# Additions moved from VectorE to GpSimd in a convolution and MLP kernel whose matmuls use seven products

## The chip, the cores and the metric

The kernel runs on one core of a Trainium2 chip. The metric is the device time of one execution in microseconds (us). The time before is the median of three runs. The five engines of the core each run their own stream of instructions in order and wait for each other by semaphores: TensorE (PE in the profile, its weight loads PEld), VectorE (DVE), ScalarE (ACT), GpSimd (POOL) and SyncE (SP), which only issues transfers here. GpSimd issues transfers too.

## The reference

The input x has the shape (8, 4224, 192) in float32. First comes a causal convolution over the sequence: the 192 channels form 8 heads of 24, each head has 7 taps, and the taps of a head go through a softmax.

```python
w = exp(weight - max); w = w / (sum(w) + 1e-9)            # (8 heads, 7 taps)
out[b, s, h, g] = sum_k w[h, k] * x_pad[b, s + k, h, g]    # 6 zeros stand ahead of x
```

Then an MLP with a layer norm ahead of it works on each row y of 192 numbers (w_ch1 is 192 x 768, w_ch2 is 768 x 192):

```python
xn = (y - mean(y)) / sqrt(var(y) + 1e-6) * g_ln
result = y + maximum(xn @ w_ch1, 0) @ w_ch2
```

## The kernel before

**Groups.** The rows are cut into 18 groups of up to 2048 rows, 16 rows (J) on each of the 128 partitions. Groups 0 and 1 run plainly. For group 2 only the second matmul, and for groups 3 to 17 (MIXED) both matmuls, are computed by seven products of quarters instead of eight, with sums and differences of quarters ahead of and behind the products. The division by the standard deviation is put off: the first weights are centred, and `rstd` multiplies the result of the second matmul.

**Convolution.** The taps of a group are added on VectorE two groups ahead of its matmuls or one: `first_tap` and `second_tap` run on ScalarE (line 380, 398), the second tap's addition is a transfer from tb to y that adds as it lands (line 409, issued by GpSimd), and `conv` (line 417) adds the taps from 2 to 6, head by head, one instruction of 128x384 for each tap and head. `transpose` (line 428) then brings y into yt for TensorE, and `moments` (line 448) takes the statistics.

**First matmul, `up_mixed(g)`.** It runs the seven products twice: a small pass (`one`, a third of the features: index PAIR) and a large pass (`two`, the other two thirds). X and Y are the two halves of the PSUM banks, used in turn: a product into X can begin only when ScalarE has copied X's last result out (`evict`, line 651). A quarter that is the sum of two results is closed by `close`: either VectorE adds PSUM to it (line 657), or ScalarE copies the second result to a free place and a transfer issued by GpSimd adds it (line 609). The free place for the small pass's c21 is `two.c22[:, 0:1]`, which the large pass later writes with its own c22; so that eviction waits until the transfer has landed. The large pass uses parts_cs and parts_tb as free places.

**Second matmul, `down_fast(g)`.** Its seven products (line 850) are called P0 to P6 here. P0 to P3 read the quarters as they are, after `lower_sum` (line 826: a10 = max(a10, 0) - a00, one VectorE instruction for each of three feature indices). P4, P5 and P6 read what three times three half sums (line 817) make of them: P4 reads the first three, and of those the one with index PAIR first, which is made last. ScalarE copies the products into cs and parts (line 856); the parts lie where a10 was. After P6 the next group begins at once.

**Behind the products.** The results of group g-1 are completed in `finish_fast` (line 908), which the generator `ahead` calls in the middle of `up_mixed(g)`: VectorE adds parts to cs (line 912) and transposes six blocks of cs into ot (line 914); ScalarE multiplies by rstd (line 929), and GpSimd issues the transfers that add ot to the output (line 940).

**Order.** The order is written out by hand; nothing reorders it. Each engine keeps the order in which the program names its instructions. What matters of it here:

- VectorE, in a group: taps of the next group, `lower_sum` of index PAIR, three more taps, the closing addition of line 657, the other two `lower_sum`, nine taps, the transpose to yt, nine half sums, three additions from PSUM (line 890), the sums of y s1 and s2 (lines 600 and 601), 16 statistics, then the two additions and six transposes of `finish_fast`.
- GpSimd: the four issues of line 409, the sums of y s3 and s4 (lines 605 and 606), in every second group a memset (line 164), then the transfers that close c11, c22 and c21 of the small pass and those of the large pass. In groups 4, 6, ... 16 (and in 17) `root` (lines 460 to 483) computes rstd for two groups: nine operations on 128x32 elements between the closings of c11 and c22, and ten between those of c22 and c21.

In `up_mixed` this is the piece around the last products:

```python
        p.product(Y, s1, p.b12, False, False)
        taps_of_next(2, 5)
        taps_of_next(5, 6, heads=(0, H // 2))
        p.close(p.c22, Y, None if last else rooms[1][:, 0:PAIR])
        p.product(X, a22, p.t[2], False)
```

Of the kernel before, what the change touches and what calls it, by code (L numbers as in the profile page):

```python
# [11 lines left out]
ALU = mybir.AluOpType  # L12
# [4 lines left out]
def kernel(  # L17
# [29 lines left out]
    nc = tc.nc  # L47
    PSUM = bass.MemoryType.PSUM
    B, S, D = x.shape
    H, K = weight.shape  # L50
# [35 lines left out]
    CH = NC // 2  # L86
# [38 lines left out]
    def take_set():  # L125
        i = (turn[0] + 3) // 4 * 4 % 8
        turn[0] = i + 4
        return all_banks[:, i : i + 4]
# [482 lines left out]
    def up_mixed(g, ahead, pending):  # L611
# [65 lines left out]
                conv(g + 1, *args, **kw)  # L677


        X, Y = take_set(), take_set()  # L680
        one, two = Pass(PAIR, FC, X, Y), Pass(0, PAIR, Y, X)
        p = one
        p.product(X, a11, p.b11, True, False)
        p.evict(X, p.c11)
        p.product(Y, a12, p.b21)
        p.close(p.c11, Y, two.c12[:, 0:1])
        next(pending, None)
        p.product(X, s2, p.t[0], False, False)
        p.evict(X, p.c21)
        p.product(Y, s3, p.t[1], True, False)  # L690
        p.evict(Y, p.c22)
        p.product(X, s1, p.b12, False, False)
        p.close(p.c22, X, two.c12[:, 1:2])
        next(pending, None)
        p.product(Y, a22, p.t[2], False)
        p.close(p.c21, Y, two.c22[:, 0:1])
        p.product(X, s4, p.b22, False)
        p.evict(X, p.c12, True)

        next(ahead)  # L700
        p = two
        rooms = parts(cpool, "cs"), parts(bpool, "tb")
        p.product(Y, a11, p.b11, True, False)
# [37 lines left out]
        if last:  # L741
            one.relu(one.c22)
        else:
            lower_sum(g, (PAIR,))
            taps_of_next(5, 6, heads=(H // 2, H - 1))
        p.close(p.c21, X)
        if last:
            lower_sum(g, (PAIR,))
# [5 lines left out]
        if last:  # L754
# [9 lines left out]
                nc.scalar.activation(kept[:, f, :, :, h], src, AF.Relu)  # L764

            keeping = [lambda f=f, h=h: keep(f, h) for f in range(NF) for h in range(2)]
        taps_of_next(5, 6, heads=(H - 1, H))
        taps_of_next(6, K)

        def scale_one(j):  # L770
# [47 lines left out]
                a[:, *dst, f], a[:, *left, f], a[:, *right, f], op=op  # L818
            )

    def lower_sum(g, fs=range(FC)):

        a = of_products(g)
        if g in MIXED:
            for f in fs:
                nc.vector.scalar_tensor_tensor(
                    out=a[:, 1, 0, f], in0=a[:, 1, 0, f], scalar=0.0, in1=a[:, 0, 0, f],
                    op0=ALU.max, op1=ALU.subtract,
                )
        else:  # L830
            half_sum(g, (1, 0), (1, 0), (0, 0), ALU.subtract, fs)

    def down_fast(g, work):
        n = fast[g]
        t = width(g)
        w = n * T
        a = of_products(g)
        flat = cpool.tile([P, NC, NFAST * C], F32, tag="cs", name=f"cs{g}")[:, :, 0 : n * C]
        order = "p c (h j t) -> p c h j t" if t == C else "p c (j h t) -> p c h j t"
        cs = flat.rearrange(order, h=2, t=t)  # L840
        free = a[:, 1, 0].rearrange("p f q j t -> p (f q) j t")
        parts = [free[:, 0:CH], free[:, CH : 2 * CH]]
        banks = [take_bank() for c in range(CH) for i in range(2)]

        def product(bank, left, right, to, first, behind=0):
            for c in range(CH):
                dst = banks[2 * c + bank]
                for f in (PAIR, *range(PAIR)):
                    for q in range(NQ):
                        nc.tensor.matmul(  # L850
                            dst[C * q : C * q + C, 0:w], right[:, f, C * c : C * c + C],
                            left[:, f, q], start=(first and f == PAIR), stop=(f == PAIR - 1),
                            skip_group_check=True,
                        )
                if to is not None:
                    nc.scalar.copy(  # L856
                        to[:, c], dst[:, 0:w].rearrange("p (j t) -> p j t", t=t)
                    )
                for one in work[:behind]:
                    one()  # L860
                del work[:behind]

        b = quarters_of_w2()
        c11, c21 = cs[:, 0:CH, 0], cs[:, 0:CH, 1]
        c12, c22 = cs[:, CH:NC, 0], cs[:, CH:NC, 1]
        if g == 2:
            work += [lambda h=h: first_tap(4, heads=(h, h + 1)) for h in range(7, H)]
            work += [lambda h=h: second_tap(4, heads=(h, h + 1)) for h in range(H)]
        elif g + 2 < NG:
            work += [  # L870
                lambda tap=tap, h=h: tap(g + 2, heads=(h, h + 1))
                for tap in (first_tap, second_tap) for h in range(H)
            ]
        behind = (1, 1, 1, 1) if g == 2 else (3, 2, 2, 3)
        if g + 1 == NG:
            behind = (0, 0, 1, 2)
        product(0, a[:, 0, 0], b[0], c11, True, behind[0])
        product(1, a[:, 1, 0], w2sums[:, 2], c22, True, behind[1])
        product(1, a[:, 1, 1], w2sums[:, 3], c21, False, behind[2])
        product(1, a[:, 0, 1], b[2], None, True, behind[3])  # L880
        if g + 1 < NG:
            transpose(g + 1)
            if g == 2:
                b11, b12 = quarters_of_w1()[0:2]
                nc.vector.tensor_tensor(b12, b12, b11, op=ALU.subtract)
        half_sum(g, (1, 1), (1, 1), (1, 0), ALU.add)
        half_sum(g, (0, 0), (1, 1), (0, 0), ALU.add)
        half_sum(g, (0, 1), (0, 1), (1, 1), ALU.subtract)
        for c in range(CH):
            nc.vector.tensor_tensor(  # L890
                c11[:, c], c11[:, c], banks[2 * c + 1][:, 0:w].rearrange("p (j t) -> p j t", t=t),
                op=ALU.add,
            )
        product(0, a[:, 1, 1], w2sums[:, 1], parts[0], False, 2)
        product(0, a[:, 0, 0], w2sums[:, 0], parts[1], False, 2)
        for one in work:
            one()
        product(0, a[:, 0, 1], b[3], c12, False)
        if g + 1 < NG:
            sums_of_y(g + 1, nc.gpsimd)  # L900
            if g == 2:
                load_x(5, gate=True)
            moments(g + 1)
        else:
            finish_fast(g, 0, flat, cs, parts)
        return flat, cs, parts

    def finish_fast(g, half, flat, cs, parts):
        n = fast[g]
        ot = ots[g] if half else out_tile(g)  # L910
        fresh = cs[:, CH * half : CH * half + CH, 1]
        nc.vector.tensor_tensor(fresh, fresh, parts[half], op=ALU.add)
        for c in range(CH * half, CH * half + CH):
            nc.vector.transpose(
                ot[:, 0:n, C * c : C * c + C], flat[:, c].rearrange("p (j t) -> p j t", t=C)
            )

    ots = {}

# [76 lines left out]
    def ahead(g):  # L996


        if results is not None:
            for half in range(2):  # L1000
                finish_fast(g - 1, half, *results)
        yield

    w11, w12, w21, w22 = quarters_of_w1()
    b11, b12, b21, b22 = quarters_of_w2()
# [100 lines left out]
```

## Time and profile before

| what | before |
|---|---|
| time, median of 3 runs (lowest to highest) | 955.75 us (955.62 to 957.78) |
| the profiled execution's own time | 956.96 us |
| its span | 954.6 us |
| TensorE busy | 946.8 us, 99% |
| VectorE busy | 894.2 us, 94% |
| ScalarE busy | 694.8 us, 73% |
| GpSimd busy | 341.8 us, 36% |
| one steady group: first matmul, second matmul | 27.96 us, 27.44 us |
| one tap on VectorE, 128x384 | 615 ns, next one 0.53 us later |
| VectorE, two inputs of 128x768, in place (L912) | 929 ns |
| GpSimd, two inputs of 128x768 (L605) | 1831 ns |

The span runs from the first to the last instruction of the profiled execution. L609 means line 609 of the kernel before. In the timeline, a line gives the start, the time that a run of like instructions took (both in us), the engine, the line, what is written and read, shapes and count; in brackets stands how long the engine was idle before, and who ended that wait.

### The profile page before, as it was taken

The page shows a single profiled execution, that of the slowest core. Times are in us where ns is not written, and L with a number is a line of the kernel's source. Part 1 is how long each engine was busy: PE and PEld are TensorE (multiplying, and loading weights), DVE is VectorE, ACT ScalarE, POOL GpSimd, SP SyncE. Part 2 cuts the span into 40 slices and gives each one's busy share as a digit, 9 for nine tenths or more (in the row PEclk, how much of TensorE's full clock was granted, in tenths as well). Part 3 has the DMA queues.
Part 4 walks back from the last instruction along what each step waited for, and adds up shares of the span by engine and source line. Part 5 has one row for each costly group of instructions (what it writes and reads, how often), then busy time and mean ns, then how long its engine had stood idle before and what let it go on. Part 6 is the DMA issues. An engine that isn't in the chain of part 4 may idle for free.

```text
span 954.6 us, 37896 instructions
## 1 busy us (share of the span) xinstructions
PE 946.8 (99%) x16858; PEld 734.5 (77%) x16858; DVE 894.2 (94%) x1496; ACT 694.8 (73%) x1166; POOL 341.8 (36%) x474
## 2 busy tenths in 40 slices
PE   8999999999999999999999999999999999999998
PEld 7998896877869687786958778695867769586787
DVE  8999999999999999999999999999999999999867
ACT  7764678596877959687796968779695877967362
POOL 1158422613145141533227141452316232261330
PEclk9999999999999999999999999999999999999999
DMA  8359589689696988979697897969889697778261
GB/s 206 111 151 218 110 233 269 122 188 226 130 273 131 251 158 185 221 130 278 126 252 152 199 215 128 277 133 249 158 198 206 124 275 134 174 135 141 40 122 68
DMA packets 39832, 169.34 MB, mean 177 GB/s; under 512 B 4469, under 2 KB 8182, under 8 KB 33655
## 3 DMA queue, kind: packets, MB, share of 16 engines
q0 software_dynamic: 32864, 106.77, 60.2%
q1 hardware_dynamic: 6800, 60.16, 17.4%
q8 instruction: 132, 2.16, 0.9%
q14 instruction: 30, 0.25, 0.1%
q10 hardware_dynamic: 6, 0.00, 0.0%
HBM read 38.93 MB, written 50.33 MB: 94 GB/s over the span
## 4 chain that ended last, share of the span: by engine, by line
PE 96%; DMA 1%; POOL 1%; ACT 1%; issue 0%; DVE 0%; ACTq 0%; POOLq 0%
PE ps L533 46%; PE ps L850 44%; PE ps L787 4%; PE ps L367 1%; DMA room<-room 1%; DMA out_dram<-y 1%; PE ps L326 1%; ACT room L651 0%; POOL room L609 0%; POOL d L460 0%; ACT y L380 0%; POOL r L483 0%; POOL d L478 0%; POOL d L479 0%; PE ps L335 0%
## 5 line engine op out<-in xcount | busy, mean ns | idle before, releaser
L417 DVE SCALAR_TENSOR_TENSOR y<-xg,taps,y 128x384 f32<-128x384 f32 (+3 forms) x720 | 364.8, 583 | 2.6 <-DMA y<-room 1.4
L850 PE MATMUL ps<-room,w2sums 128*32 128x256 f32 (+2 forms) x4608 | 246.6, 371 | 0.0
L533 PE MATMUL ps<-yt,w 32*128 32x256 f32 (+2 forms) x4104 | 234.7, 378 | 1.0 <-ACT room L523 0.5
L533 PEld LDWEIGHTS ps<-yt,w 32*128 32x128 f32 x4104 | 204.2, 185 | 26.3 <-issue 8.7
L651 ACT COPY room<-ps 128x1024 f32<-128x1024 f32 (+1 forms) x129 | 169.0, 1310 | 74.5 <-PE ps L533 73.5
L850 PEld LDWEIGHTS ps<-room,w2sums 128*32 128x32 f32 x4608 | 149.3, 110 | 91.5 <-ACT room L664 5.3
L850 PE MATMUL ps<-room,w 128*32 128x256 f32 (+2 forms) x3456 | 188.9, 371 | 0.0
L817 DVE TENSOR_TENSOR room<-room 128x1024 f32<-128x1024 f32 (+2 forms) x147 | 161.2, 1170 | 22.6 <-PE ps L850 16.0
L850 PEld LDWEIGHTS ps<-room,w 128*32 128x32 f32 x3456 | 110.7, 110 | 70.3 <-DVE room L657 5.0
L533 PE MATMUL ps<-ysums,w1sums 32*128 32x256 f32 x2160 | 124.9, 379 | 0.2 <-issue 0.2
L533 PEld LDWEIGHTS ps<-ysums,w1sums 32*128 32x128 f32 x2160 | 109.5, 185 | 10.5 <-ACT room L651 3.3
L940 POOL DMA_DIRECT2D out_dram<-ot x69 | 59.0, 942 | 155.6 <-ACT ot L929 102.5
L409 POOL DMA_DIRECT2D y<-tb x59 | 52.5, 1386 | 153.5 <-ACT room L856 110.1
L856 ACT COPY cs<-ps 128x256 f32<-128x256 f32 (+2 forms) x192 | 70.1, 367 | 45.2 <-PE ps L850 45.2
L664 ACT ACTIVATE room<-room 128x1024 f32<-128x1024 f32 (+1 forms) x89 | 92.5, 1072 | 1.7 <-DMA room<-parts_cs 0.9
L929 ACT ACTIVATE ot<-ot,r 128x192 f32<-128x192 f32 x224 | 90.9, 464 | 0.0
L380 ACT ACTIVATE y<-xg,taps 128x384 f32<-128x384 f32 (+3 forms) x141 | 73.0, 607 | 1.0 <-DMA out_dram<-y 0.7
L448 DVE BATCH_NORM_STATS2 st<-y 128x6 f32<-128x192 f32 x264 | 70.1, 344 | 0.0
L856 ACT COPY room<-ps 128x256 f32<-128x256 f32 (+2 forms) x96 | 35.5, 370 | 45.8 <-PE ps L850 43.8
L398 ACT ACTIVATE tb<-xg,taps 128x384 f32<-128x384 f32 (+1 forms) x120 | 66.1, 628 | 0.0
L533 PE MATMUL ps<-yt,w1sums 32*128 32x256 f32 x1080 | 65.2, 380 | 0.6 <-ACT room L651 0.6
L533 PE MATMUL ps<-ysums,w 32*128 32x256 f32 x1080 | 64.5, 376 | 0.0
(119 smaller groups left out, 924.8 us busy)
## 6 DMA issues: line engine op xcount, KB each, us to landing
xg<-in_x_dram SPq DMA_DIRECT2D x14, 2112.0 KB, 16.4
room<-room POOLq DMA_DIRECT2D x45, 512.0 KB, 5.1
out_dram<-ot POOLq DMA_DIRECT2D x59, 384.0 KB, 9.6
y<-tb POOLq DMA_DIRECT2D x58, 384.0 KB, 8.4
out_dram<-y SPq DMA_DIRECT2D x13, 1536.0 KB, 8.8
room<-parts_cs POOLq DMA_DIRECT2D x28, 512.0 KB, 6.7
room<-parts_tb POOLq DMA_DIRECT2D x14, 1024.0 KB, 7.6
xg<-in_x_dram POOLq DMA_DIRECT2D x1, 2112.0 KB, 13.8
```

What stands on the lines that cost most here:

```text
L380: nc.scalar.mul(y[g][:, 0:n, cs], xg[g][:, 0:n, cs], taps[:, h, 0:1])
L398: nc.scalar.mul(tb[g][:, 0:n, cs], xg[g][:, 1 : 1 + n, cs], taps[:, h, 1:2])
L417: nc.vector.scalar_tensor_tensor(out=y[g][:, 0:n, cs], in0=t[:, k : k + n, cs], scalar=taps[:, h, k : k + 1], in1=y[g][:, 0:n, cs], op0=AL ...
L448: nc.vector.bn_stats(out=sums[g][:, j, :], in_=y[g][:, j, :])
L533: nc.tensor.matmul(banks[:, q, i * w : i * w + w], right[rows, c, P * i : P * i + P], left[rows, :, c, :], start=(first and c == 0 and i = ...
L651: nc.scalar.activation(dst, src, AF.Relu) if relu else nc.scalar.copy(dst, src)
L664: nc.scalar.activation(c, c, AF.Relu)
L817: nc.vector.tensor_tensor(a[:, *dst, f], a[:, *left, f], a[:, *right, f], op=op)
L850: nc.tensor.matmul(dst[C * q : C * q + C, 0:w], right[:, f, C * c : C * c + C], left[:, f, q], start=(first and f == PAIR), stop=(f == PAI ...
L856: nc.scalar.copy(to[:, c], dst[:, 0:w].rearrange("p (j t) -> p j t", t=t))
L929: nc.scalar.mul(ots[g][:, j, :], ots[g][:, j, :], rstd[g][:, j : j + 1])
L940: nc.gpsimd.dma_start(out=rows[:, d0:d1], in_=src[:, d0:d1], accum_op=ALU.add)
```

## The change

1. `add_parts` takes the two additions of parts to cs out of `finish_fast`; in all groups but the last they run on GpSimd at the end of `down_fast`, one ahead of and one behind the sums s3 and s4.
2. The six transposes become a generator that is advanced one step after each eviction of the small pass, and drained after it. In the last group it is only drained.
3. `lower_sum` of index PAIR runs on GpSimd, as a clamp at zero and a subtraction, in all groups of seven-product first matmuls but the last.
4. The three taps that stood between that `lower_sum` and the closing addition (line 657) now stand behind that addition.

```diff
+        def some_of_last():
+            if not last:
+                next(ahead, None)
+
         X, Y = take_set(), take_set()
         one, two = Pass(PAIR, FC, X, Y), Pass(0, PAIR, Y, X)
         p = one
         p.product(X, a11, p.b11, True, False)
         p.evict(X, p.c11)
+        some_of_last()
         p.product(Y, a12, p.b21)
         p.close(p.c11, Y, two.c12[:, 0:1])
+        some_of_last()
         next(pending, None)
...
         p.product(Y, a22, p.t[2], False)
         p.close(p.c21, Y, two.c22[:, 0:1])
+        some_of_last()
         p.product(X, s4, p.b22, False)
         p.evict(X, p.c12, True)
 
-        next(ahead)
+        for _ in ahead:
+            pass
         p = two
...
         if last:
             one.relu(one.c22)
         else:
-            lower_sum(g, (PAIR,))
-            taps_of_next(5, 6, heads=(H // 2, H - 1))
+            lower_sum(g, (PAIR,), nc.gpsimd)
         p.close(p.c21, X)
...
-        taps_of_next(5, 6, heads=(H - 1, H))
+        taps_of_next(5, 6, heads=(H // 2, H))
         taps_of_next(6, K)
...
-    def lower_sum(g, fs=range(FC)):
+    def lower_sum(g, fs=range(FC), engine=nc.vector):
 
         a = of_products(g)
         if g in MIXED:
             for f in fs:
+                if engine is nc.gpsimd:
+                    low = a[:, 1, 0, f]
+                    engine.tensor_scalar(
+                        out=low, in0=low, scalar1=0.0, scalar2=0.0, op0=ALU.max, op1=ALU.add
+                    )
+                    engine.tensor_tensor(low, low, a[:, 0, 0, f], op=ALU.subtract)
+                    continue
                 nc.vector.scalar_tensor_tensor(
...
         product(0, a[:, 0, 1], b[3], c12, False)
         if g + 1 < NG:
+            add_parts(0, cs, parts, nc.gpsimd)
             sums_of_y(g + 1, nc.gpsimd)
+            add_parts(1, cs, parts, nc.gpsimd)
             if g == 2:
                 load_x(5, gate=True)
             moments(g + 1)
...
-    def finish_fast(g, half, flat, cs, parts):
+    def add_parts(half, cs, parts, engine):
+        fresh = cs[:, CH * half : CH * half + CH, 1]
+        engine.tensor_tensor(fresh, fresh, parts[half], op=ALU.add)
+
+    def transposes_of_last(g, half, flat, cs, parts):
         n = fast[g]
         ot = ots[g] if half else out_tile(g)
-        fresh = cs[:, CH * half : CH * half + CH, 1]
-        nc.vector.tensor_tensor(fresh, fresh, parts[half], op=ALU.add)
         for c in range(CH * half, CH * half + CH):
             nc.vector.transpose(
                 ot[:, 0:n, C * c : C * c + C], flat[:, c].rearrange("p (j t) -> p j t", t=C)
             )
+            yield
+
+    def finish_fast(g, half, flat, cs, parts):
+        add_parts(half, cs, parts, nc.vector)
+        for _ in transposes_of_last(g, half, flat, cs, parts):
+            pass
...
         if results is not None:
             for half in range(2):
-                finish_fast(g - 1, half, *results)
-        yield
+                yield from transposes_of_last(g - 1, half, *results)
```

More of the change, by code (lines that the diff above doesn't have):

```diff
@@ L689, in up_mixed @@
         p.evict(X, p.c21)
+        some_of_last()
         p.product(Y, s3, p.t[1], True, False)
         p.evict(Y, p.c22)
+        some_of_last()
         p.product(X, s1, p.b12, False, False)
         p.close(p.c22, X, two.c12[:, 1:2])
+        some_of_last()
         next(pending, None)
@@ L696, in up_mixed @@
         p.close(p.c21, Y, two.c22[:, 0:1])
+        some_of_last()
         p.product(X, s4, p.b22, False)
         p.evict(X, p.c12, True)
-        next(ahead)
+        for _ in ahead:
+            pass
         p = two
```

## The prediction

> **What bounds it.** I read the page first: busy times, then the chain that ended last.
>
> ```profile
> PE 946.8 (99%) x16858; PEld 734.5 (77%) x16858; DVE 894.2 (94%) x1496; ACT 694.8 (73%) x1166; POOL 341.8 (36%) x474
> ...
> PE 96%; DMA 1%; POOL 1%; ACT 1%; issue 0%; DVE 0%; ACTq 0%; POOLq 0%
> ```
>
> TensorE is without work for 7.8 us of 954.6; by the table by stretches 3.1 of them fall in the first 30 us, 0.8 between 117.2 and 894.3 (groups 3 to 16), the rest at the very end. VectorE's 94% is nobody's bound. So taking work off VectorE can return almost nothing; the question is which result for TensorE comes later. The chain in order of time shows groups of exactly 27.96 + 27.44 = 55.40 us and one disturbance:
>
> ```profile
> 671.86 27.96 PE ps L533 x504
> 699.82 27.44 PE ps L850 x504
> ...
> 741.88 6.76 DMA room<-room
> ...
> 748.74 1.88 ACT room L651
> 750.61 0.04 issue
> 750.66 5.46 PE ps L533 x96
> ```
>
> In group 14 the transfer closing the small pass's c21 (L609), issued last behind `root`'s operations on GpSimd, landed 6.76 us later and held ScalarE's eviction, which held TensorE: the stage took 28.86 by the table by stretches, 0.90 more. A weak spot to remember. The timeline of the end of group 11's first matmul and of its second one:
>
> ```profile
> 586.07 0.86 POOL L609 DMA_DIRECT2D room<-parts_tb  x1 [6.85 <-ACT parts_tb L651]
> 586.56 2.29 DVE L657 TENSOR_TENSOR room<-room,ps 128x2048 f32<-128x2048 f32 x1 [0.85 <-PE ps L533]
> 588.95 2.36 DVE L826 SCALAR_TENSOR_TENSOR room<-room 128x1024 f32<-128x1024 f32 x2
> 591.23 4.85 DVE L417 SCALAR_TENSOR_TENSOR y<-xg,taps,y 128x384 f32<-128x384 f32 x9
> 596.21 3.38 DVE L428 STREAM_TRANSPOSE yt<-y 128x3072 f32<-128x3072 f32 x1
> 600.61 10.31 DVE L817 TENSOR_TENSOR room<-room 128x1024 f32<-128x1024 f32 x9 [1.03 <-PE ps L850]
> 604.62 7.95 PE L850 MATMUL ps<-room,w2sums 128*32 128x256 f32 x144
> ```
>
> VectorE waits twice: 0.85 for TensorE before the closing addition (L657), 1.03 before the half sums (L817). P4, the matmul at 604.62, reads the third half sum first; that ends at 600.61 + 3 x 1.146 + 0.06 = 604.1 (10.31/9 = 1.146), and VectorE to TensorE takes 0.1 (588.85 to 588.95). So 0.42 is spare.
>
> [...]
>
> ```profile
> 72.21 9.02 DVE L417 SCALAR_TENSOR_TENSOR y<-xg,taps,y 128x384 f32<-128x384 f32 x12
> 71.27 3.16 POOL L582 TENSOR_TENSOR w2sums<-w 128x288 f32<-128x288 f32 x2
> 74.51 2.07 POOL L582 TENSOR_TENSOR w2sums<-w,w2sums 128x288 f32<-128x288 f32 x2
> ```
>
> Twelve taps cost 12 x 0.53 = 6.4 elsewhere (28 in 14.87); beside four GpSimd additions of 288 elements, 9.02: 0.65 lost for each. [...] Trace: 768 elements take 1.83 (L605) against 0.95 (L600) for two inputs; of one input only 32-element operations are there (0.21).
>
> **Part 1: lower sum to GpSimd, three taps behind the closing.** Leaves VectorE: one L826, 1.2 us, before L657; worth nothing, VectorE waited 0.85 there and will now wait about 3. The three taps (1.6) that also stood before L657 now stand behind it, where the spare is 1.03: 0.57 late at the half sums, so 0.57 - 0.42 = 0.15 of TensorE.
>
> On GpSimd: a clamp and a subtraction of 1024 elements, behind the parts_tb issue, which ends at 586.93. Subtraction: from 0.25 at 32 elements to 1.83 at 768, 2.15 ns each, so 2.4. Clamp, one input: estimate 1.1[...]; bounds 1.1 and 2.4. It runs 586.95 to 588.05 beside L657, which has one SBUF input, the other in PSUM. The subtraction starts at 588.05, [...]and VectorE's first L826, due at 588.95, waits 1.4. P1 wants the result at 592.85 (588.95 + 3.90): in time. Behind it on GpSimd stand only the stores of the rows of ot, first issued at 593.16: not delayed. The half sums are then 1.4 + 1.6 - 1.03 = 1.97 late, P4 1.97 - 0.42 = **1.5 us** in each odd group 3 to 15.
>
> **Part 2: the two additions to GpSimd.** VectorE loses 2 x 0.93 (L912) per group, again before a wait. GpSimd gains 2 x 1.83, the same shape as L605. They enter here (group 14; its start S is 727.19):
>
> ```profile
> 724.77 1.83 POOL L605 TENSOR_TENSOR ysums<-yt 128x768 f32<-128x768 f32 x1 [0.46 <-PE ps L850]
> 726.68 1.82 POOL L606 TENSOR_TENSOR yt<-yt,ysums 128x768 f32<-128x768 f32 x1
> 728.44 1.05 POOL L164 MEMSET xg<- 1x1152 f32 x1
> 731.44 0.90 POOL L609 DMA_DIRECT2D room<-room  x1 [1.95 <-ACT room L651]
> ```
>
> Both wait for ScalarE's copies of the parts, the last of which ends at S-3.4 (L856, 612.64 + 0.37 in group 11, whose successor starts at 616.39): no wait. The first comes after the y<-tb issues (to S-2.9) and meets VectorE's sums of y (L600, L601, two SBUF inputs): one of them waits, so L605 starts at about S-0.3 instead of S-2.4. L605 and L606 end at S+3.4, wanted by TensorE at about S+4.1 and S+8.3 (s3 by 1.9, s4 by L606): hidden. The second addition ends at S+5.2. Before even groups the memset follows: S+6.3. Behind it queue the c11 closing (before S+4.25), nine `root` operations, the c22 closing (S+8.4), ten more, the c21 closing (S+14.69). In odd groups there is no `root`: c11 closes 1 us late, c21 at S+9.9 as before; free.
>
> In even groups the queue is full. Nine operations took 3.5 (732.05 to 735.53) because seven ran beside one-input transposes; beside taps their pitch is 0.55 (735.57 to 741.88 for ten and an issue, 6.3). VectorE's transposes wait for the second addition, so its taps start at S+7.3 to 7.7 (before S+7.1), and about seven operations run slowly: S+6.3, issue 0.6, 4.4 to 5, then 6.3: c21 is issued at S+17.7 (3 later). Landing took 4.65 in a quiet case (187.7, group 4), 6.76 in group 14; with the parts_cs transfers now right behind it I take 5.3: S+23.0. The eviction that waits for it normally starts at S+20.45, so 2.6 late, and group 14 shows 1.09 late cost 0.90: **2.5 us** per even group 4 to 16. Bounds: 1.4 (issue at S+17.3, landing in 4.65) and 4.2. There parts_tb is issued some 0.95 ahead of L657 instead of 0.5, which shortens part 1 to **1.0**.
>
> **Part 3: order of the transposes.** Their order in VectorE's stream does not change (nothing else of VectorE's stands in the small pass, except in the last group, where the generator is drained at the old place): 0, bounded by the 1.9 that half of them take, covered by VectorE's wait of 3 us at L657.
>
> **Sum.** 7 x 1.5 + 7 x (1.0 + 2.5) - 0.9 already paid = 34. The last group keeps its sum on VectorE: 0. Profiled span 954.6 becomes 989; that execution took 956.96, 1.2 above the median, so I add 34 to the median 955.75: **990**.
>
> **Rivals.** (a) One of the two stalls alone, 22%: c21 lands in time (+21, 977), or part 1 is only 0.15 and part 2 whole (+19, 975). For: each hangs on slacks of 0.4 to 1.2. Against: the queue's extra work is certain. (b) The clamp is as slow as the subtraction, or L657 counts as a contender: two holds instead of one, 3.1 in odd and 2.6 in even groups: 7 x 3.1 + 7 x 5.1 - 0.9 = 56, 1012; 17%. No large one-input operation is in the trace to exclude it. (c) Not slower, 6%: GpSimd's long operations don't hold VectorE at L826 and L600. Then part 1 is 0.15 x 14 = 2.1, s3 starts at S-2, c21 is issued at S+15.9 and lands at S+20.5, no later than needed: about 957. It decides if the hold at L826 is below 0.42 - 0.15 = 0.27 us; the 0.65 per 288 elements speaks against it. (d) Faster, 2%: the 0.8 us between 117.2 and 894.3 is all that these edits could return.
>
> **How the numbers follow.** The rest, 53%, is the forecast, its own range 980 to 1000. 968 leaves (c), (d) and a corner of (a) below; 1014 leaves the half of (b) where both holds are long above. A measurement here tells changes over 0.3% (2.9 us) from none: faster 0.02, within 0.06, slower 0.92.
>
> **What would show it.** L843's first instruction starts after GpSimd's subtraction ends, not 2.39 after L657's start; L827 no longer waits for TensorE; P4 (L867) waits for VectorE. In even groups L651 waits for room<-room by some 2.5 us, and the third L609 is issued near S+17.7. VectorE waits about 3 us before L657. Wrong if P4 starts 15.67 after P0 as now, or if the c21 closing stays near S+15.

## The result, and the profile after

| what | before | after |
|---|---|---|
| time, median of 4 runs (lowest to highest), same chip | 956.22 us (955.62 to 957.78) | 1015.0 us (1012.72 to 1019.61) |
| ratio, 95% interval | | 1.0618 (1.0578 to 1.0658) |
| profiled execution: time, span | 956.96, 954.6 us | 1012.72, 1010.9 us |
| groups 3 to 16, first matmul | 27.96 us, 28.38 in group 3, 28.86 in group 14 | 27.96 us in odd groups (group 3 as before), 28.2 to 32.3 in even ones but group 16 |
| groups 3 to 16, second matmul | 27.44 us, 27.62 in group 6 | 29.55 us in 8 groups, 30.31 in group 3, 32.4 to 34.0 in 5 |

The kernel became 58.8 us slower. The direction was as forecast, the size was not: 990 was forecast, with 1014 as the upper end. The loss lies in TensorE's waits, and to a small part (4.3) in the half clock behind some of them. The page of the kernel after, its busy times and the engines of the chain that ended last:

```profile
PE 958.6 (95%) x16858; PEld 734.9 (73%) x16858; DVE 911.2 (90%) x1452; ACT 697.4 (69%) x1166; POOL 494.6 (49%) x532
...
PE 54%; POOL 19%; DVE 14%; issue 6%; DMA 4%; ACT 3%; SPq 0%; POOLq 0%; DVEq 0%; ACTq 0%
```

Before, 96% of that chain was TensorE; now a third of it is GpSimd and VectorE. VectorE executes 44 instructions fewer than before and is busy 17 us longer: the records of held instructions are longer (in group 11, below, twelve taps 8.56 instead of 6.4, nine half sums 14.01 instead of 10.3). The waits of the kernel after (who waited for whom: us in total, times, longest):

```profile
PE ps L867 <- DVE room L827: 31.3, 19, 2.7
...
ACT room L651 <- DMA room<-room: 8.3, 6, 3.0
...
PE ps L867 <- POOL room L841: 7.1, 13, 0.6
PE ps L533 <- ACT room L651: 6.1, 5, 2.6
```

L867 is the line of the products P0 to P6 (L850 before), L827 that of the half sums (L817), L838 and L841 the clamp and the subtraction on GpSimd, L843 the lower sums left on VectorE (L826), L929 an addition of parts (L912). TensorE waits for half sums 19 times in 14 groups: 14 times at P4, as forecast, and 5 times at another place. It waits 13 times for the subtraction itself, which was forecast to be in time. The second and the last row, ScalarE for a transfer and TensorE for ScalarE, are the late c21. The timeline of group 11 (start, us, engine, line, what is written and read, count, idle time before and its releaser), in which all of them but the late c21 are to be seen:

```profile
619.06 2.29 DVE L657 TENSOR_TENSOR room<-room,ps 128x2048 f32<-128x2048 f32 x1 [3.57 <-PE ps L533]
619.12 3.96 POOL L838 TENSOR_SCALAR room<-room 128x1024 f32<-128x1024 f32 x1
...
621.44 2.36 DVE L843 SCALAR_TENSOR_TENSOR room<-room 128x1024 f32<-128x1024 f32 x2
623.17 2.87 POOL L841 TENSOR_TENSOR room<-room 128x1024 f32<-128x1024 f32 x1
623.72 8.56 DVE L417 SCALAR_TENSOR_TENSOR y<-xg,taps,y 128x384 f32<-128x384 f32 x12
...
626.10 7.98 PE L867 MATMUL ps<-room,w2sums 128*32 128x256 f32 x144 [0.56 <-POOL room L841]
...
635.69 14.01 DVE L827 TENSOR_TENSOR room<-room 128x1024 f32<-128x1024 f32 x9
...
639.20 7.98 PE L867 MATMUL ps<-room,w2sums 128*32 128x256 f32 x144 [1.24 <-DVE room L827]
...
643.24 3.54 POOL L409 DMA_DIRECT2D y<-tb  x4 [9.08 <-ACT tb L398]
...
645.43 3.18 POOL L929 TENSOR_TENSOR cs<-cs,room 128x768 f32<-128x768 f32 x1
...
649.85 2.37 PE L867 MATMUL ps<-room,w 128*32 128x256 f32 x40 [2.67 <-DVE room L827]
```

Four things are to be read here. The clamp (L838) takes 3.96, not 1.1, and ends at 623.08. Both L843 run beside it and take what they took before, 2.36 for two: the clamp holds neither of them. The record of the subtraction starts at 623.17, 0.6 before the second L843 ends (623.80), and the first of the twelve taps meets it: those twelve take 8.56, where 6.4 is normal, so the hold is 2.1. The subtraction ends at 626.04, and P1 (626.10), which could have begun at about 625.5, waits for it: 0.56. P4 (639.20) then waits for the half sums. And the nine half sums take 14.01 instead of 10.3: the ninth is held beside L409's issues and L929, and P6 waits 2.67 for it.

The late c21 is seen in group 6, which starts at S = 292.74:

```profile
310.09 0.89 POOL L609 DMA_DIRECT2D room<-room  x1
...
316.28 1.86 ACT L651 COPY room<-ps 128x2048 f32<-128x2048 f32 x1 [2.99 <-DMA room<-room]
```

The closing of c21 is issued at S+17.35, and ScalarE's eviction waits 2.99 for it to land.

The same place as in group 11, but in group 5, where P6 did not wait:

```profile
277.43 10.27 DVE L827 TENSOR_TENSOR room<-room 128x1024 f32<-128x1024 f32 x9
...
284.99 3.53 POOL L409 DMA_DIRECT2D y<-tb  x4 [9.09 <-ACT tb L398]
...
287.17 3.21 POOL L929 TENSOR_TENSOR cs<-cs,room 128x768 f32<-128x768 f32 x1
...
288.61 2.59 DVE L600 TENSOR_TENSOR ysums<-yt 128x768 f32<-128x768 f32 x1
```

The half sums are whole, and the hold falls on the sum of y behind them (L600, 2.59 instead of 0.95), for which TensorE does not wait. In the records of single instructions, in group 5 as in group 9, the ninth half sum starts 1.50 after the first L409 issue and L929 starts 2.18 after it; it took 1.22 in group 5 and 4.97 in group 9. The start times that the trace gives don't tell which VectorE instruction is held; it was the ninth half sum in five groups (6, 9, 11, 12, 15). Group 3 belongs to them in part: there the issues end earlier, the addition starts before the ninth half sum, and that one takes 2.85 and ends at 171.69. P6 starts at 171.84, and this second matmul loses 0.8 more than those without a wait at P6 (the profile puts this wait down to a copy by ScalarE).

Last, stretches of the kernel after, behind a wait at P6 in group 11 and behind one in group 12 (busy time of the engines with instruction counts in brackets, granted clock, DMA share, GB/s):

```profile
649.85:653.80 3.95, 3.95 (x72) 2.67 (x72) 3.92 (x12) 0.75 (x2) 1.08 (x1) 1.00 1.07 205
710.45:713.40 2.95, 2.95 (x28) 1.54 (x32) 2.92 (x8) 0.11 (x1) 0.07 (x1) 0.50 1.08 207
```

In group 12 TensorE runs at half its clock for these 2.9 us: 28 matmul instructions in 2.95 against 72 in 3.95. This costs about 1.4 and happens three times (behind P6's wait in groups 9 and 12, behind the wait for c21 in group 6).

Added up by stages of the profiled execution, the fastest of the four, against the kernel before: 14 groups by 2.11 at P1 and P4, 29.5; the five waits at P6, 2.9 to 4.4 each with the half clock in two of them, 17.4; the first matmuls, 8.9 (group 6: 4.3 with the half clock, group 4: 1.9, the rest up to 1.0); 0.8 more in group 3's second matmul. Together 56.6; the spans differ by 56.3. Only this execution of the kernel has a trace, so in how many groups P6 waits in the others is not known.

### The profile page after: what moved, and what is told of

It reads as the page before. It is cut to its first block, busy times and chain, and to the rows that moved or that the text cites. A ratio compares the mean times of both kernels' runs of the same rounds, so it can differ in the third digit from the quotient of the medians.

```text
span 1010.9 us, 37979 instructions
## 1 busy us (share of the span) xinstructions
PE 958.6 (95%) x16858; PEld 734.9 (73%) x16858; DVE 911.2 (90%) x1452; ACT 697.4 (69%) x1166; POOL 494.6 (49%) x532
## 4 chain that ended last, share of the span: by engine, by line
PE 54%; POOL 19%; DVE 14%; issue 6%; DMA 4%; ACT 3%; SPq 0%; POOLq 0%; DVEq 0%; ACTq 0%
PE ps L533 26%; PE ps L867 24%; DVE room L827 11%; POOL room L838 5%; POOL room L841 4%; PE ps L797 4%; DMA room<-room 3%; ACT parts_tb L651 2%; POOL d L460 1%; POOL ysums L605 1%; POOL yt L606 1%; POOL cs L929 1%; POOL room L609 1%; DMA xg<-in_x_dram 1%; POOL r L483 1%
## 5 line engine op out<-in xcount | busy, mean ns | idle before, releaser
L417 DVE SCALAR_TENSOR_TENSOR y<-xg,taps,y 128x384 f32<-128x384 f32 (+3 forms) x720 | 391.4, 618 | 2.5 <-DMA y<-room 1.4
L867 PE MATMUL ps<-room,w2sums 128*32 128x256 f32 (+2 forms) x4608 | 245.7, 371 | 25.1 <-DVE room L827 18.0
L867 PEld LDWEIGHTS ps<-room,w2sums 128*32 128x32 f32 x4608 | 146.7, 110 | 123.3 <-DVE room L827 24.8
L867 PE MATMUL ps<-room,w 128*32 128x256 f32 (+2 forms) x3456 | 192.1, 375 | 13.9 <-DVE room L827 13.3
L827 DVE TENSOR_TENSOR room<-room 128x1024 f32<-128x1024 f32 (+2 forms) x147 | 180.9, 1304 | 8.3 <-ACT kept L774 6.6
L867 PEld LDWEIGHTS ps<-room,w 128*32 128x32 f32 x3456 | 112.9, 111 | 86.3 <-issue 18.6
L409 POOL DMA_DIRECT2D y<-tb x59 | 52.3, 1378 | 162.1 <-ACT tb L398 162.1
L657 DVE TENSOR_TENSOR room<-room,ps 128x2048 f32<-128x2048 f32 x16 | 36.6, 2288 | 71.5 <-PE ps L533 45.4
L929 POOL TENSOR_TENSOR cs<-cs,room 128x768 f32<-128x768 f32 (+1 forms) x30 | 73.8, 2460 | 10.7 <-ACT room L873 10.7
L533 PE MATMUL ps<-yt,w1sums 32*128 32x256 f32 x1080 | 67.5, 387 | 6.1 <-ACT room L651 6.1
## 6 DMA issues: line engine op xcount, KB each, us to landing
xg<-in_x_dram SPq DMA_DIRECT2D x14, 2112.0 KB, 16.1
```

What stands on the lines that cost most here:

```text
L417: nc.vector.scalar_tensor_tensor(out=y[g][:, 0:n, cs], in0=t[:, k : k + n, cs], scalar=taps[:, h, k : k + 1], in1=y[g][:, 0:n, cs], op0=AL ...
L533: nc.tensor.matmul(banks[:, q, i * w : i * w + w], right[rows, c, P * i : P * i + P], left[rows, :, c, :], start=(first and c == 0 and i = ...
L827: nc.vector.tensor_tensor(a[:, *dst, f], a[:, *left, f], a[:, *right, f], op=op)
L867: nc.tensor.matmul(dst[C * q : C * q + C, 0:w], right[:, f, C * c : C * c + C], left[:, f, q], start=(first and f == PAIR), stop=(f == PAI ...
L929: engine.tensor_tensor(fresh, fresh, parts[half], op=ALU.add)
```

## The experiments

Each time stands beside that of the kernel before on the same chip. In the expectations H (later R, Q, T and W) is my theory as it stood, and the other letters are its rivals. In the diffs, lines are taken out of or put into the kernel after, unless the kernel before is named; variants of part 1 or of part 2 carry the diff of that part alone besides their own.

**Part 1 alone** (`part1_only`): lower sum on GpSimd and taps behind the closing; the additions are VectorE's again.

```diff
-            add_parts(0, cs, parts, nc.gpsimd)
             sums_of_y(g + 1, nc.gpsimd)
-            add_parts(1, cs, parts, nc.gpsimd)
...
     def transposes_of_last(g, half, flat, cs, parts):
+        if g + 1 < NG:
+            add_parts(half, cs, parts, nc.vector)
```

> Part 1 alone: the lower sum of index PAIR on GpSimd and the three taps behind the closing addition; the two additions of parts are back on VectorE. Theory H[...]: GpSimd's subtraction holds VectorE's taps for 2.1 us in each of 14 groups, P1 and P4 wait together 2.1 us, so +29 us (about 985), the second matmul 29.55 in every group, no wait of P6, first matmul 27.96. Rival A (the additions on GpSimd are what makes the half sums late): about 957 to 962.

985.51 us against 957.24, ratio 1.0295 (1.0274 to 1.0317): 28.3 us. Each second matmul takes 29.57 to 29.59, each first one 27.96 (28.39 in group 3, 28.19 in group 14), and P6 never waits. So the 2.1 per group is part 1's, in even groups as in odd ones, and the wait at P6 needs the additions.

**Part 2 alone** (`part2_only`): the additions on GpSimd, lower sum and taps where they were.

```diff
-            lower_sum(g, (PAIR,), nc.gpsimd)
+            lower_sum(g, (PAIR,))
+            taps_of_next(5, 6, heads=(H // 2, H - 1))
         p.close(p.c21, X)
...
-        taps_of_next(5, 6, heads=(H // 2, H))
+        taps_of_next(5, 6, heads=(H - 1, H))
```

> Part 2 alone: the two additions of parts on GpSimd; lower sum and taps as before. Theory H: the first addition meets the ninth half sum only because part 1 has made the half sums late, so here P6 doesn't wait and the second matmul stays 27.44; even groups lose about 1 to 2 us at the c21 closing behind root, so +7 to +12 us (963 to 968). Rival B (the parts add up, each with its own cost): P6 waits in about 5 groups here too, +22 to +28 us (978 to 984).

974.46 us, ratio 1.0177 (1.0154 to 1.02): 17.2 us, more than H gave and less than B: a miss of both. The second matmuls are as before, as H said. Even groups from 8 on take 29.6 to 30.6 in the first matmul (group 4: 28.24, group 6: 33.27, with half clock), because c21 is issued at about S+18.0 and lands at S+22.7 in groups 8, 10 and 12; the prediction had S+17.7 and S+23.0. Odd groups take 0.36 more, at L657: VectorE reaches its taps late, at S+8.47, because L600 is held. The timeline of part 2 alone, VectorE and GpSimd behind a second matmul:

```profile
341.24 4.35 DVE L600 TENSOR_TENSOR ysums<-yt 128x768 f32<-128x768 f32 x1
...
341.56 3.21 POOL L930 TENSOR_TENSOR cs<-cs,room 128x768 f32<-128x768 f32 x1
```

This is the meeting of the first addition with a sum of y that the prediction named, but VectorE loses 3.4 in it, not up to 1.8. Parts 1 and 2 alone sum to 45.5; the whole costs 58.8. The excess is the wait at P6, which exists only with both, less a smaller loss in the first matmuls (8.9 instead of some 18).

**The taps alone** (`taps_only`), in the kernel before:

```diff
             lower_sum(g, (PAIR,))
-            taps_of_next(5, 6, heads=(H // 2, H - 1))
         p.close(p.c21, X)
...
-        taps_of_next(5, 6, heads=(H - 1, H))
+        taps_of_next(5, 6, heads=(H // 2, H))
```

> Only the three taps stand behind the closing addition; all lower sums and additions on VectorE. Theory H: 1.6 us more on VectorE behind the closing against 1.03 + 0.42 spare, so 0.1 to 0.2 us per group, +1.5 to +3 us (957 to 959). Rival C (the moved taps are the bulk of part 1): +15 us or more.

957.16 us, ratio 0.9998 (0.9987 to 1.0009). No cost; each second matmul is 0.01 longer. The half sums were 0.57 late by the prediction's working, so P4 had at least 0.56 to spare, not 0.42.

**The order of the transposes alone** (`order_only`), the generator in the kernel before:

```diff
         p.evict(X, p.c11)
+        some_of_last()
         p.product(Y, a12, p.b21)
...
-        next(ahead)
+        for _ in ahead:
+            pass
```

> Only the generator that gives the transposes one by one; additions, lower sum and taps as before. Each engine's order stays the same, so 0 (within 0.3%) by every theory; if waits are set earlier by it, a few us either way.

956.73 us, ratio 0.9998 (0.9989 to 1.0007): nothing, as forecast.

**Part 1 with the taps at their old place** (`part1_taps_back`):

```diff
             lower_sum(g, (PAIR,), nc.gpsimd)
+            taps_of_next(5, 6, heads=(H // 2, H - 1))
         p.close(p.c21, X)
...
-        taps_of_next(5, 6, heads=(H // 2, H))
+        taps_of_next(5, 6, heads=(H - 1, H))
```

> Part 1 alone with the three taps back ahead of the closing addition. Theory H: the hold of 2.1 us stays but VectorE has 1.6 us less behind the closing, so the half sums are about 0.5 us late; P1 still waits 0.7 us for GpSimd's subtraction and that covers it: 0.7 to 0.8 us in each of 14 groups, +10 us (965 to 969). Rival C (the taps don't matter next to the hold): about 985.

965.45 us against 957.30, ratio 1.0086 (1.0066 to 1.0105). The second matmul takes 28.10, 0.66 more than before (29.48 in group 8, its cause is open). Its timeline (L868 are the products, L842 is the subtraction):

```profile
600.18 7.98 PE L868 MATMUL ps<-room,w2sums 128*32 128x256 f32 x144 [0.56 <-POOL room L842]
...
611.86 7.95 PE L868 MATMUL ps<-room,w2sums 128*32 128x256 f32 x144
```

P1 waits as in the whole change, P4 no more. The taps that cost nothing alone cost 20 us on top of the hold. This closes the sum: VectorE is late at the half sums by the hold plus the three taps less its old wait, and P4 forgives some 0.59 (the value that makes part 1 alone come out; the taps alone asked for at least 0.56). With both, 2.13 + 1.6 - 1.03 - 0.59 = 2.11; with the hold alone 0.51, less than the 0.66 by which P1 already moved P4, so P4 has no wait of its own; with the taps alone below zero.

**Part 1 without the clamp** (`part1_no_clamp`): GpSimd subtracts only.

```diff
                 if engine is nc.gpsimd:
                     low = a[:, 1, 0, f]
-                    engine.tensor_scalar(
-                        out=low, in0=low, scalar1=0.0, scalar2=0.0, op0=ALU.max, op1=ALU.add
-                    )
                     engine.tensor_tensor(low, low, a[:, 0, 0, f], op=ALU.subtract)
```

> Part 1 alone with GpSimd's clamp left out (the subtraction works on unclamped numbers; nothing else is left out). The 2.4 us subtraction then runs beside the closing addition L657, which has one input in PSUM. Theory H[...]: no hold, no wait of P1 or P4, about 957 (956 to 960). Rival L (L657 counts as a contender too, so the subtraction begins after it and is held against the lower sums): about 985 as part 1 alone.

960.52 us, ratio 1.0034 (1.0018 to 1.005), 0.5 above H's range; the second matmul takes 27.68, 0.24 more. Its timeline (L838 is the subtraction, L840 VectorE's lower sums):

```profile
591.22 2.29 DVE L657 TENSOR_TENSOR room<-room,ps 128x2048 f32<-128x2048 f32 x1 [3.92 <-PE ps L533]
591.28 2.70 POOL L838 TENSOR_TENSOR room<-room 128x1024 f32<-128x1024 f32 x1
...
593.60 2.60 DVE L840 SCALAR_TENSOR_TENSOR room<-room 128x1024 f32<-128x1024 f32 x2
```

The subtraction lies wholly beside L657 but for its last 0.4; L657 takes its normal 2.29, and L840 loses 0.24. So the subtraction costs VectorE 0.24 where it runs beside L657, which has one input in PSUM, and 2.1 where the clamp pushes it behind L657. That L657 contends is ruled out.

**Part 1 with a clamp of one operation** (`part1_one_op`):

```diff
-                        out=low, in0=low, scalar1=0.0, scalar2=0.0, op0=ALU.max, op1=ALU.add
+                        out=low, in0=low, scalar1=0.0, scalar2=None, op0=ALU.max
```

> Part 1 alone with the clamp as one operation (max with 0, no added zero). If GpSimd's price goes with the number of operations, the clamp takes about 2 us instead of 3.96; the subtraction then starts right behind L657 and holds the second-pass lower sums instead of the taps. Theory H: P1's wait of 0.7 us goes, but VectorE loses the same 2.1 us ahead of the half sums, so P4 waits 2.1 us and the time stays about 985. Rival E (the late lower sum at P1 is the cause): about 966 to 975. If the clamp stays at 3.96, nothing changes and this tells nothing of H and E.

992.83 us, ratio 1.0372 (1.0354 to 1.0389): slower than part 1 alone by 7, where about 985 was expected. Its timeline:

```profile
491.96 3.11 POOL L838 TENSOR_SCALAR room<-room 128x1024 f32<-128x1024 f32 x1
...
494.28 4.56 DVE L843 SCALAR_TENSOR_TENSOR room<-room 128x1024 f32<-128x1024 f32 x2
...
495.15 2.60 POOL L841 TENSOR_TENSOR room<-room 128x1024 f32<-128x1024 f32 x1
```

The clamp takes 3.11, still longer than a subtraction. The hold of 2.2 moves from the first tap to the second L843; P1 no longer waits, P4 waits the more (2.0 to 2.4), and the second matmul takes 29.65 in ten groups: the same loss at one place instead of two (by the sum above 2.2 + 1.6 - 1.03 - 0.59 = 2.18; measured 2.21). In the other four (3, 7, 11, 16) it takes 31.3, and there TensorE runs at half its clock behind P4's wait: 1.7 each, 6.8 in all, most of the difference to part 1 alone (7.2). A shorter clamp made the kernel slower by making one wait long enough for that.

**What decides on the half clock** (`part1_one_op_again`): the same kernel once more, no diff. In the first trace the four P4 waits that are followed by half clock start at 160.52, 392.84, 624.97 and 915.03. Divided by 3.413 us they leave 0.09, 0.31, 0.32 and 0.26, and none of the other ten leaves a remainder between them. 3.413 is not fitted to them. It is the length of each of the three stretches of half clock in the granted clock of the whole change, which start at 317.712, 529.338 and 710.245: 211.63 and 180.91 apart, 62 and 53 times 3.4133.

> Part 1 with the one-operation clamp once more, to see which waits are followed by half clock. W (a free-running window of 3.413 us decides): P4 waits with a gap of about 2.38 in all groups as before; taken modulo 3.413 us, the starts of those waits that are followed by half clock lie together in one arc of at most 0.6 with none of the others in it, and the half clock ends at one phase, within 0.25; which groups these are, and how many (1 to 5 of 14), may differ from the first time (groups 3, 7, 11, 16). F (something in the work of these groups decides): again the groups 3, 7, 11 and 16, whatever their phase. N (chance): the waits followed by half clock and the others are mixed in phase.

One execution, 993.65 us, beside 958.25 for the kernel before. This time groups 4, 9 and 13 have it, so the groups' work does not decide. Their waits start at remainders 1.38, 0.99 and 1.34, the other eleven at none between 0.99 and 1.38. The half clock begins at 0.37, 0.45 and 0.34 and ends at 0.30, 0.39 and 0.56, one window later (the ends lie 0.01 further apart than expected). In group 9 TensorE even runs its first half microsecond behind the wait at full rate, until 0.45 comes. Worked out more finely (with 3.4133), from the spacing of the matmuls across the change of rate, the ends agree far better: by this estimate they lie at 0.48 to 0.49 for these three, 2.80 to 2.81 for the four of the first trace and 0.29 for the three of the whole change. (The granted clock of the whole change puts its three at 0.27.) So in these three traces the clock changes at the edges of such a window, and a wait, from the start of the last matmul ahead of it to the first behind it, counts by its largest piece between two edges. That piece was 2.38 or more wherever half clock followed, and 2.32 or less wherever it did not. Stretches behind the waits of groups 4, 9 and 10 (columns as above; group 10 stays at full clock):

```profile
222.21:225.35 3.14, 3.14 (x32) 1.68 (x36) 3.14 (x3) 1.19 (x4) 0.00 (x0) 0.52 1.01 338
512.70:515.90 3.20, 3.20 (x36) 1.58 (x32) 3.20 (x4) 1.48 (x4) 0.00 (x0) 0.50 1.02 357
571.27:574.40 3.13, 3.13 (x60) 1.92 (x64) 3.13 (x3) 2.38 (x6) 0.00 (x0) 1.00 1.03 345
```

The whole change fits this: of its six waits near 3 us, the three with half clock start at remainders 0.86 to 1.20, the others at 1.37 and later, where the edge at 0.29 leaves pieces of 2.32 and less.

**The whole change, both additions behind the sums s3 and s4** (`adds_behind_sums`):

```diff
-            add_parts(0, cs, parts, nc.gpsimd)
             sums_of_y(g + 1, nc.gpsimd)
+            add_parts(0, cs, parts, nc.gpsimd)
             add_parts(1, cs, parts, nc.gpsimd)
```

> The whole change, but the first addition of parts stands behind GpSimd's two sums of y, not ahead of them. Theory R (race): the addition can no longer be in flight at the ninth half sum, so P6 waits nowhere, nor does TensorE run at half clock behind that wait; part 1's 29 us and the late c21 closings (7 to 16 us) stay: 992 to 1002. Rival B (P6's waits come from the half sums being late in themselves): about 1015 as the whole change.

999.26 us, ratio 1.0445 (1.0426 to 1.0465), 42.0 us over the kernel before. P6 waits nowhere, and every second matmul but group 6's (29.63) takes 29.55; even groups take 1.2 to 2.2 more than 27.96 in the first matmul, group 6 takes 4.3 more. Against the whole change 16.8 us are gone by the medians and 13.7 by the profiled spans: the 17.4 at P6 and the 0.8 of group 3, less some 4 that the first matmuls lose more, above all in groups 10, 12 and 16. So the place of the first addition, between the issues and the sums, makes that wait.

**Part 2 with the first addition alone** (`one_addition`); the second is VectorE's again:

```diff
             sums_of_y(g + 1, nc.gpsimd)
-            add_parts(1, cs, parts, nc.gpsimd)
...
     def transposes_of_last(g, half, flat, cs, parts):
+        if half and g + 1 < NG:
+            add_parts(half, cs, parts, nc.vector)
```

> Part 2 with the first addition of parts alone on GpSimd; the second is on VectorE, lower sum and taps as before. Theory Q (queue): without the second addition's 1.8 us ahead of the memset and root, the c21 closing of even groups is issued near S+15 to S+16 and lands about in time; 0 to 0.5 us per even group, and 0 to 0.3 in odd ones by VectorE's late taps: +1 to +6 us (958 to 963). Rival D (the first addition, which holds VectorE's sums of y for over 3 us and so starts GpSimd's own sums late, is the whole delay): about 970 to 974 as part 2 alone.

970.29 us against 957.48, ratio 1.0138 (1.0119 to 1.0156): a miss, 958 to 963 was expected. The queue did what was expected: c21 is issued at S+15.9, lands at about S+20.6 and costs next to nothing (even groups take less than 0.1 more than odd ones). But from group 5 on every group, odd or even, takes some 1.2 more at L657, because L600 is held for 3.2 and VectorE comes to its taps at S+9.3 instead of S+7.1. Timeline of this kernel:

```profile
395.08 4.14 DVE L600 TENSOR_TENSOR ysums<-yt 128x768 f32<-128x768 f32 x1
```

**Part 2 with both additions behind the sums** (`part2_behind`) follows from that miss: if the held L600 is the cause, odd groups must cost nothing.

```diff
-            add_parts(0, cs, parts, nc.gpsimd)
             sums_of_y(g + 1, nc.gpsimd)
+            add_parts(0, cs, parts, nc.gpsimd)
             add_parts(1, cs, parts, nc.gpsimd)
```

> Part 2 alone, both additions of parts on GpSimd but both behind its two sums of y, as in the run with the whole change. Theory T (an addition that starts while the issues of line 409 are still under way holds VectorE until those are done, 3.4 us instead of 1.8): here no issue is under way, VectorE's sums of y aren't held, taps start near S+7.1 and VectorE waits about 0.8 us at L657 in odd groups, so odd groups cost 0; even ones 1 to 1.7 us at the c21 closing as GpSimd's queue is still full: +6 to +12 us (963 to 969). Rival D (the additions themselves make VectorE late): odd groups lose 0.3 us and more, +15 us or more (972 and up).

964.57 us against 956.40, ratio 1.0084 (1.0064 to 1.0105). Odd groups take 27.96 again, and L600 is whole in its timeline:

```profile
337.64 0.95 DVE L600 TENSOR_TENSOR ysums<-yt 128x768 f32<-128x768 f32 x1
```

Even groups still lose 0.3 to 1.9, with c21 issued at S+15.9 to S+17.1. So the additions cost through two ways, the held L600 and the queue ahead of c21, and the order on GpSimd removes only the first.

**The work left out** (`left_out`): the kernel before without the additions and without the lower sum of index PAIR, which bounds what relief of VectorE can bring.

```diff
         else:
-            lower_sum(g, (PAIR,))
             taps_of_next(5, 6, heads=(H // 2, H - 1))
...
-        nc.vector.tensor_tensor(fresh, fresh, parts[half], op=ALU.add)
+        if g + 1 == NG:
+            nc.vector.tensor_tensor(fresh, fresh, parts[half], op=ALU.add)
```

> The kernel before with work left out: the two additions of parts and the lower sum of index PAIR aren't made at all in groups 3 to 16 (the additions also not for group 2's results), on no engine. VectorE has 3.1 us less per group, about 44 in all. Theory H (TensorE alone sets the time): 0 to -1 us (955 to 958). Rival V (VectorE's 94% is part of the bound): -15 us or more.

960.56 us, ratio 1.0034 (1.0023 to 1.0046): no gain with the work gone altogether, even a loss of 3.1, where at most a gain of 1 was expected. VectorE comes to its taps at S+5.1 to S+5.6, so more of `root` runs beside taps, and c21 is issued as late as S+16.4; groups 4, 14 and 16 lose 0.7 to 1.9 there (group 14's 0.9 was lost in the kernel before too). (Groups 6 and 13 lose 1.3 and 0.5 in the second matmul; the cause is open.)

No version was found that beats the kernel before.

## Why the prediction was right in direction and too low

| step of the prediction | forecast, us | measured, us |
|---|---|---|
| part 1: P1 "in time", P4 1.5 in odd and 1.0 in even groups | 17.5 | 29.5 (14 x 2.11) |
| part 2: c21 2.5 in even groups, less 0.9 already paid | 16.6 | 8.9 |
| the first addition "comes after the y<-tb issues (to S-2.9) and meets VectorE's sums of y" | 0 | 17.4 at P6, of which 2.9 is half clock |
| the same step in group 3's second matmul, beyond 2.11 (by the timeline) | 0 | 0.8 |
| order of the transposes | 0 | 0 |

The misses add up to the whole one: 12.0 too little for part 1, 18.2 put at nothing for the first addition, 7.7 too much for c21, together 22.5 between 34.1 and 56.6. That part 2 was put too high hid a quarter of the other two; this was luck.

**The bound** held. TensorE alone set the time; leaving out VectorE's work gained nothing, and VectorE now waits 3.57 at L657 in group 11 where about 3 was forecast.

**Part 1: the mechanism was right, the clamp mis-sized.** The hold by the subtraction, the late half sums and the wait at P4 are there. The price of the clamp, "estimate 1.1", with bounds of 1.1 and 2.4, failed: it takes 3.96. The 1.1 was my estimate; the largest one-input GpSimd instruction in the trace before has 128 elements, not 32, and takes 0.33 (L311), so nothing of this size showed it. That the subtraction holds a VectorE instruction to its own end was my estimate too; in group 11 its record ends 2.32 after the first tap's start, and the hold is 2.13. From the clamp's price follow the other misses of this part. The subtraction starts 4.1 after L657 and not 1.5 (588.05), so the hold is 2.13 and not 1.4, and it falls on the first tap; the sign that L843's first instruction would start behind the subtraction did not come. P1, "in time", waits 0.56; and the even groups' 1.0 fell too, since they lose the same 2.11. P4's spare was 0.59 instead of 0.42, which took back a little.

**Part 2: the queue was right, its size near, and the change moved it.** Alone, part 2 measures 17.2, near the forecast's 16.6, but by luck in part: not all of it is c21, 0.36 per odd group comes from the held L600, and the half clock in group 6 is in it. In the whole change c21 is issued at S+16.1 to S+17.35 (S+15.0 in group 16) and the first matmuls lose 8.9. P4's wait delays S, but not ScalarE's taps, so the y<-tb issues run at S-7.75 instead of S-6.42 and the first addition starts earlier by the group's clock.

**The step that was wrong in its place** is where the first addition lands. The prediction timed it as for part 2 alone, with part 1's stall absent. With that stall the issues come earlier against the half sums, and in five groups the addition meets the ninth half sum, which P6 reads, instead of a sum of y. A hold that TensorE does not see became one that it does. The prediction added the two parts as if independent; they are not.

**The rivals.** (b) came nearest in number, 1012, with the clamp as slow as the subtraction. But it derived that number from two holds per group, and only one is there: beside the clamp L657 keeps its 2.29 and the two L843 their 2.36, and beside the subtraction alone L657 keeps its 2.29 again. The rest came from P6; that its number came near is chance. (a), one stall alone, is out: both are there. (c), not slower, and (d), faster, are out by the hold of 2.1 and by the kernel with the work left out.

**Not foreseen:** the half clock behind some waits, 4.3 in all. It is contained in the rows above: 2.9 at P6 and 1.4 in group 6's first matmul.

## What to carry to other kernels

Here TensorE was busy for 99% of the span, and even leaving VectorE's work out returned nothing (960.56 beside 957.48). So ask first whether the engine that is relieved sets the time, and follow each moved instruction to what stands behind it in its new queue and to what it runs beside there: the same subtraction cost VectorE 0.24 us beside L657 and 2.1 behind it. Add up stalls only after shifting the later ones by the earlier ones: P4's wait moved the y<-tb issues from S-6.42 to S-7.75 against the group's clock, and a meeting that TensorE did not see became one that it does, 17.4 in all. Keep the upper bound of an instruction that the trace does not show well above the two-input price until it is measured: the clamp took 3.96, and its upper bound of 2.4 was the forecast for the subtraction.

## What the runs showed of the hardware that I had not expected

- GpSimd's `tensor_scalar` on 128x1024 float32 takes 3.96 us with two operations (3.958 to 3.979 in 14 instances) and 3.11 with one, more than the two-input subtraction of the same size (mostly 2.6 to 2.9 beside VectorE's work). Each of these clamps ran beside L657 and L843; no run times one with VectorE idle, so how much of it is waiting stays open.
- The clamp with two operations ran beside VectorE's two L843, which have two SBUF inputs; they kept their 2.36. The subtraction did hold VectorE behind a clamp, for 2.1 to 2.2.
- An addition of 768 elements that is started while GpSimd's own transfer issues (L409) are still under way takes 3.2 instead of 1.8, and VectorE's instruction beside it was held by 3.2 to 3.8 where it met the whole of it (L600 4.14 and 4.35 instead of 0.95; a half sum 4.97 instead of 1.22). In 38 such additions (the whole change, part 2 alone, the first addition alone) the record ends 1.83 to 1.87 after the last issue's, and 1.8 is an addition's usual length. The traces keep the two apart: with the additions behind the sums, the same issues run beside half sums that take their normal 1.22; in group 16 of part 2 alone, where no issue is near, L600 takes 1.60 (the addition's own record is 3.40 there, as it runs into two half sums first). So neither alone makes the long hold; by what means the two together make it was not shown.
- TensorE runs at half its clock for about 3 us behind some waits of 2.4 to 3.3 us (granted clock 0.50 in the stretch 710.45:713.40). It depends on where the wait lies against a free-running window of 3.413 us (in the whole change three stretches of half clock, each 3.413 long, start 62 and 53 such lengths apart), and so on chance; waits up to 2.2 never had it. In the three traces 2.38 us of one window were enough and 2.32 were not.
